# All large backward transfers issued from SyncE in program order, with dV up to eight heads ahead of dK and dq moved forward

## The chip, the cores and the metric

The kernel runs on one core of one Trainium2 chip. The metric is the device time of one execution in microseconds. The core has five engines with an instruction stream of their own (TensorE or PE, VectorE or DVE, ScalarE or ACT, GpSimd or POOL, SyncE or SP) and 16 DMA engines, which move data between the chip's main memory (HBM) and the on-chip memory (SBUF). Any of SyncE, ScalarE and GpSimd can issue a DMA; the issue stands in that engine's stream like any other instruction, and waits there for what it depends on.

## What is computed

One decoding step (one new token for each of B = 4 sequences) of a transformer layer, forward and backward. All tensors are bf16. Attention has H = 32 heads of Dh = 128 and a cache of Sk = 4096 keys and values; D = 512, F = 1792.

```python
def _A_ref(x, k_cache, v_cache, wq, wo):
    q = (x @ wq) split into heads
    scores = einsum("bhqd,bhkd->bhqk", q, k_cache) * Dh ** -0.5
    p = softmax(scores)
    o = einsum("bhqk,bhkd->bhqd", p, v_cache)
    return o.reshape(B, 1, H * Dh) @ wo
def _B_ref(x, w1, w3, w2):
    return (silu(x @ w1) * (x @ w3)) @ w2
h = x + _A_ref(layernorm(x), k_cache, v_cache, wq, wo)
out = h + _B_ref(layernorm(h), w1, w3, w2)
```

The outputs are `out` and the gradients of a loss with the given `grad_out` with respect to x, k_cache, v_cache, wq, wo, w1, w3 and w2. The two cache gradients, dK and dV, have the size of the caches, 134 MB each, and they and the caches make nearly all of the traffic: K is read once, V twice, dK and dV are written once. For each of the 128 pairs of sequence and head (called heads below, s = 0 to 127), with P the softmax row, q the query, dO the gradient of the head's output row, dV = P (outer) dO, dS = P * (V dO - c) * scale, and dK = dS (outer) q.

## The kernel before

**Tiling.** A head's K, V, dK or dV is 4096 rows of 128 numbers, 1 MB in bf16. It lies in SBUF as 128 partitions of 32 rows, 8 KB a partition, in one of 23 equal slots (`NSLOT`, class `Slot`). A slot is taken from the front of the list `free` and given back to its end when the program no longer writes to it; the framework then makes its next user wait until the old one is done. Which slot is used when is thus settled when the program is built.

**Stages.** The forward part (L614 to L676) takes two heads a turn: K and V loads from SyncE, scores, softmax, and per head a 128 x 129 matrix M (sum over the keys of V times P K, and the output column), eight slots `Ms` of 16 heads. Then comes a short middle part (L800 to L924): the feed-forward block and its gradients, dh, the first 8 of 32 head columns of dO, and dV of heads 0 and 1. The rest, from L927, is the backward loop.

**The backward loop (L1218 to L1246).** `front(s)` (L1161) transposes V in four pieces on TensorE (`V_T`, L757; the matmuls are L764, ScalarE's copies back into the same slot L765), and multiplies it with dO (L1177, `dP_ps`; the small stationary `zd` is copied by GpSimd at L1142). Four heads make a group: `rows_out` and `rows_T` bring the group's row through ScalarE (L1152) and TensorE (L1159) into shape, `group_dS` (L1185) makes dS of four heads on VectorE (L1191, L1194). `grad_V(s)` (L777) and `grad_K(s)` (L1197) each take a slot, fill it on VectorE with one outer product (L770, one instruction over 128 x 4096) and store it. They need the rows of dO and q spread over all partitions: `replicate` (L1121; matmuls L1128, ScalarE copies L1131) does that for four heads of both at a time, into two buffers each. dV also needs a doubled copy of P, `P_pairs` (L1144), made by GpSimd at L1147 into three buffers.

Step s of the loop does: load of V ahead, `replicate(s + 4)` in every fourth step, `P_pairs(s + 5)`, `front(s + 5)`, `grad_V(s + 3)`, `grad_K(s)`, in every fourth step `group_dS`, and a piece of other work. V for the backward part lies in a ring of seven slots (`NV2`): a slot goes back to the ring after its head's `front`, and the next load into it is issued one step later.

**Who issues what in the backward part.** V loads: ScalarE (`load_V2(nc.scalar)`, L1206 and L1214). dV stores: GpSimd (L781). dK stores: SyncE (L1201). Stores of weight gradients: GpSimd (L1026, L1069, L1085, L1096). Loads of wq (L961) and w2 (L502): SyncE.

**The other work** is written as generators, and `step(k, n)` runs n pieces. `rest_of_dO` ("o", one piece in each of the steps from `O0` = 2 to 20) transposes the rest of wo, and makes the rest of dO. `side_work` ("s", three pieces in steps 21 to 35, then two) begins with dq: for each of the 128 heads a matmul of M with dO in fp32 (L964), three heads a piece, after which M's slots are given back one by one. Then follow wq transposes and dx, and the weight gradients (`grad_unit`, one matmul and one ScalarE copy at L940 a piece; a slot full of them is stored).

Of the kernel before, what the change touches and what calls it, by code (L numbers as in the profile page):

```python
# [9 lines left out]
FP32 = mybir.dt.float32  # L10
# [14 lines left out]
def kernel(  # L25
# [751 lines left out]
    def grad_V(s):  # L777
# [3 lines left out]
        nc.gpsimd.dma_start(out=rows_of(out_3[b, h]), in_=gv.heads())  # L781
# [145 lines left out]
    with ExitStack() as c2:  # L927
# [22 lines left out]

        def side_work():
# [3 lines left out]
            dq_ps = psx.tile([P, 512], FP32, tag="x2", name="dq_ps")  # L955
            wq2s = deque()

            def load_wq2(cc):
                if cc < DC:
                    wq2s.append(Slot("wq2"))  # L960
                    nc.sync.dma_start(out=wq2s[-1].b(HD), in_=A_wq[cc * P:(cc + 1) * P, :])  # L961

            for s in range(NH):
                nc.tensor.matmul(dq_ps[:, s:s + 1], lhsT=M_of(s)[:, 0:Dh], rhs=dOT_f[:, s:s + 1], start=True, stop=True)  # L964
                if s % MC == MC - 1:
                    Ms[s // MC].give()
                    if s // MC in (3, 5):
                        load_wq2(s // MC // 2 - 1)
                if s % 3 == 2:
                    yield  # L970
# [46 lines left out]
            for cc in range(DC):  # L1017
# [8 lines left out]
                nc.gpsimd.dma_start(out=out_4[cc * P:(cc + 1) * P, :], in_=st.b(HD))  # L1026
# [35 lines left out]
            for i in range(2):  # L1062
# [6 lines left out]
                nc.gpsimd.dma_start(out=out_8[i * 7 * P:(i + 1) * 7 * P, :].rearrange("(p c) j -> p c j", c=7),  # L1069
# [5 lines left out]
            for (rows, out_ap) in ((dg_rows, out_6), (du_rows, out_7)):  # L1075
                for i in range(2):
# [8 lines left out]
                    nc.gpsimd.dma_start(out=out_ap[i * 2 * P:(i + 1) * 2 * P, :].rearrange("(p c) f -> p c f", c=2),  # L1085
# [3 lines left out]
            for h0 in range(0, H, 8):  # L1089
# [6 lines left out]
                nc.gpsimd.dma_start(out=out_5[h0 * P:(h0 + 8) * P, :].rearrange("(p k) j -> p k j", k=8),  # L1096
# [24 lines left out]
        def replicate(i0):  # L1121
            K_ = 8 * B if i0 < 8 * B else P
            for nm_, rows in (("rdo", dOrows_bf), ("rq", qrows_bf)):
                if (nm_, i0 // REP) in reps:
                    continue
                ps = psrep.tile([P, REP, Dh], FP32, tag="rep", name="rep_ps")
                for i in range(REP):
                    nc.tensor.matmul(ps[:, i, :], lhsT=ident_b[0:K_, i0 + i:i0 + i + 1].to_broadcast([K_, P]), rhs=rows[0:K_, :],  # L1128
                                     start=True, stop=True)
# [74 lines left out]
        def prefetch():  # L1204
            while nv["next"] < NH and vring:
                load_V2(nc.scalar)  # L1206
# [70 lines left out]
```

## Time and profile before

| | |
|---|---|
| median of 14 runs | 1716.83 us (1712.33 to 1720.81) |
| the profiled execution | 1714.46 us |
| its span in the profile | 1712.5 us, mean TensorE clock 0.88 |
| busy: PE, DVE, ACT, POOL | 73%, 72%, 57%, 28% of the span |
| moved by DMA | 707.49 MB, mean 413 GB/s |
| read from HBM, written | 422.59 MB, 282.34 MB |
| V loads of the backward part | 119 from ScalarE, 9 from SyncE |
| issue to landing, median | V load 15.6 us, dK store 15.8 us, dV store 29.2 us |
| one dV or dK on VectorE (L770) | 2.30 us, 2.29 us |

The profile gives, for each engine, when each instruction ran and what ended the idle time before it; for the DMA engines, the mean share of time in which they were busy and the rate at which they moved data. The span is cut into 40 equal slices, 42.8 us each: slices 1 to 16 hold the forward part, the hand-over lies in the seventeenth, and the rest is the backward loop. Stretches of time are in us from the start of the span. An engine that is idle costs nothing by itself; what matters is which work ends last, and what it waited for.

### The profile page before, as it was taken

The page shows a single profiled execution, that of the slowest core. Times are in us where ns is not written, and L with a number is a line of the kernel's source. Part 1 is how long each engine was busy: PE and PEld are TensorE (multiplying, and loading weights), DVE is VectorE, ACT ScalarE, POOL GpSimd, SP SyncE. Part 2 cuts the span into 40 slices and gives each one's busy share as a digit, 9 for nine tenths or more (in the row PEclk, how much of TensorE's full clock was granted, in tenths as well). Part 3 has the DMA queues.
Part 4 walks back from the last instruction along what each step waited for, and adds up shares of the span by engine and source line. Part 5 has one row for each costly group of instructions (what it writes and reads, how often), then busy time and mean ns, then how long its engine had stood idle before and what let it go on. Part 6 is the DMA issues. An engine that isn't in the chain of part 4 may idle for free. (4 is left out here: it accounts for less than half of the span.)

```text
span 1712.5 us, 38306 instructions
## 1 busy us (share of the span) xinstructions
PE 1252.7 (73%) x16180; PEld 927.1 (54%) x16180; DVE 1229.2 (72%) x1294; ACT 968.0 (57%) x1502; POOL 471.5 (28%) x822
## 2 busy tenths in 40 slices
PE   5889888888888888766689875665766666656660
PEld 4777677667666666644467754443444433434330
DVE  5989999999998996466767457475556464665684
ACT  3556445444544454676664466675776756656660
POOL 1211232222222221122332244254323131211140
PEclk9999999999999999899886689887797777887895
DMA  9999999999999999799999999999999999999997
GB/s 401 424 424 424 424 424 424 424 423 423 415 424 411 423 408 395 306 394 426 425 426 425 426 386 425 412 425 423 424 423 421 422 409 420 422 422 423 423 425 303
DMA packets 101740, 707.49 MB, mean 413 GB/s; under 512 B 11052, under 2 KB 15288, under 8 KB 17600
## 3 DMA queue, kind: packets, MB, share of 16 engines
q1 hardware_dynamic: 63568, 432.04, 60.5%
q0 software_dynamic: 20864, 148.22, 20.7%
q10 hardware_dynamic: 17136, 124.79, 17.7%
q8 instruction: 127, 2.08, 0.5%
q14 instruction: 45, 0.37, 0.1%
HBM read 422.59 MB, written 282.34 MB: 412 GB/s over the span
## 5 line engine op out<-in xcount | busy, mean ns | idle before, releaser
L765 ACT COPY V<-pt_tps 128x1024 bf16<-128x1024 bf16 x512 | 490.2, 1026 | 166.2 <-PE pt_tps L764 115.2
L764 PE MATMUL pt_tps<-ident_b,V 128*128 128x128 bf16 x4096 | 356.6, 248 | 208.2 <-ACT V L765 202.3
L764 PEld LDWEIGHTS <-V 128*128 128x128 bf16 x4096 | 305.0, 113 | 270.8 <-issue 257.4
L770 DVE TENSOR_TENSOR gv<-P,reps 128x4096 bf16<-128x4096 bf16 x125 | 287.1, 2297 | 129.4 <-DMA out_dram<-gv 110.8
L770 DVE TENSOR_TENSOR gk<-dS,reps 128x4096 bf16<-128x4096 bf16 x128 | 292.7, 2289 | 105.3 <-DMA out_dram<-gv 72.6
L421 DVE TENSOR_TENSOR PK<-Kn,PK 128x4096 bf16<-128x4096 bf16 x128 | 292.3, 2283 | 26.3 <-POOL PK L417 25.9
L436 PE MATMUL M_ps<-PK,Vn 128*128 128x130 bf16 x4096 | 284.1, 221 | 34.9 <-DMA Vn<-in_A_v_cache_dram 34.2
L436 PEld LDWEIGHTS <-Vn 128*128 128x128 bf16 x4096 | 251.8, 99 | 55.3 <-DMA Vn<-in_A_v_cache_dram 47.5
L328 DVE STREAM_TRANSPOSE KT<-Kn 128x512 f32<-128x512 f32 (+1 forms) x321 | 250.6, 797 | 0.3 <-issue 0.2
L1177 PE MATMUL dP_ps<-V,zd 128*32 128x512 bf16 x1024 | 182.3, 440 | 75.2 <-ACT V L765 63.0
L323 ACT COPY KT<-pt_tps 128x1024 bf16<-128x1024 bf16 x128 | 129.5, 1012 | 187.7 <-PE pt_tps L322 154.1
L781 POOL DMA_DIRECT2D out_dram<-gv x128 | 68.2, 533 | 490.3 <-DVE gv L770 464.3
L417 POOL COPY PK<-P_all 128x64 bf16<-128x64 bf16 x128 | 32.4, 253 | 414.9 <-ACT P_all L411 411.9
L334 POOL TENSOR_TENSOR W<-qrep,wmask 128x128 bf16<-128x128 bf16 x128 | 123.6, 966 | 82.3 <-PE S_ps L354 67.7
L1147 POOL COPY P<-P_all 128x64 bf16<-128x64 bf16 x127 | 138.1, 1088 | 0.0
L1177 PEld LDWEIGHTS <-zd 128*32 128x32 bf16 x1024 | 37.6, 95 | 163.3 <-issue 137.2
L1191 DVE TENSOR_SCALAR dPr<-dPT_ps,c_rep 128x32 f32<-128x32 f32 x128 | 23.2, 244 | 131.1 <-PE dPT_ps L1159 130.9
L1142 POOL COPY zd<-dOT_bf 128x2 bf16<-128x2 bf16 x128 | 85.2, 666 | 79.5 <-PE dP_ps L1177 79.5
L1131 ACT CAST reps<-rep_ps 128x512 bf16<-128x512 f32 x62 | 36.3, 586 | 112.7 <-DVE gk L770 74.2
L411 ACT COPY P_all<-pt_P 32x64 bf16<-32x64 bf16 x256 | 51.9, 203 | 53.6 <-PE pt_P L407 51.3
L322 PE MATMUL pt_tps<-ident_b,Kn 128*128 128x128 bf16 x1024 | 80.9, 224 | 0.0
L446 PE MATMUL kP_ps<-PK,onesw 128*32 128x512 bf16 x1024 | 79.1, 386 | 0.0
(244 smaller groups left out, 1359.2 us busy)
## 6 DMA issues: line engine op xcount, KB each, us to landing
Kn<-in_A_k_cache_dram SPq DMA_DIRECT2D x128, 1024.0 KB, 15.5
Vn<-in_A_v_cache_dram SPq DMA_DIRECT2D x128, 1024.0 KB, 15.7
out_dram<-gv POOLq DMA_DIRECT2D x128, 1024.0 KB, 29.2
out_dram<-gk SPq DMA_DIRECT2D x128, 1024.0 KB, 15.8
V<-in_A_v_cache_dram ACTq DMA_DIRECT2D x119, 1024.0 KB, 15.6
V<-in_A_v_cache_dram SPq DMA_DIRECT2D x9, 1024.0 KB, 18.9
wq<-in_A_wq_dram SPq DMA_DIRECT2D x8, 1024.0 KB, 19.5
out_dram<-gw POOLq DMA_DIRECT2D x6, 896.0 KB, 42.2
```

Source lines behind the costliest of these rows:

```text
L322: nc.tensor.transpose(pt[:, i, :], Kn[:, c * GW + i, :], ident_b[:])
L323: nc.scalar.copy(out=KT[:, c * GW:(c + 1) * GW, :], in_=pt[:])
L328: nc.vector.transpose(out=KT[:, c * w_:(c + n) * w_], in_=Kn[:, c * w_:(c + n) * w_])
L334: nc.gpsimd.tensor_tensor(out=W[:, hl], in0=qrep[:, :, s:s + 1].to_broadcast([P, 4, 32]), in1=wmask[:, hl, None, :].to_broadcast([P, 4, 32 ...
L421: nc.vector.tensor_tensor(out=PK[:, :, 0:Dh].rearrange("p j (r t) -> p j r t", t=2), in0=Ks[s].heads().rearrange("p j (r t) -> p j r t", t=2),
L436: nc.tensor.matmul(hold["M"][:], lhsT=Vn[:, j, :], rhs=PK[:, j, :], start=(j == 0), stop=(j == SJ - 1))
L764: nc.tensor.transpose(pt[:, i, :], v[:, g * GW + i, :], ident_b[:])
L765: nc.scalar.copy(out=v[:, g * GW:(g + 1) * GW, :], in_=pt[:])
L770: nc.vector.tensor_tensor(out=dst.rearrange("p j (r t) -> p j r t", t=2), in0=col2[:, :, None, :].to_broadcast([P, SJ, Dh // 2, 2]), in1=r ...
L1142: nc.gpsimd.tensor_copy(out=zd[s % B][:, 32:132:67], in_=dOT_bf[:, s:s + 1].to_broadcast([P, 2]))
L1147: nc.gpsimd.tensor_copy(out=P2s[s][:], in_=P_all[:, s, :, None].to_broadcast([P, SJ, 2]))
L1177: nc.tensor.matmul(rows["acc"][32 * c:32 * (c + 1), :], lhsT=zq_window(zd[hl], 2 * hl + u), rhs=VT[:, j0:j0 + 4, :], start=(hl == 0 and u ...
```

## The change

Three things are changed.

- Where large transfers are issued. The V loads of the backward loop, the dV stores and the weight gradient stores are issued from SyncE, which already issues the dK stores. They stand in its stream in the order in which the program writes them. GpSimd keeps only small DMAs, ScalarE none.
- How far dV runs ahead. `more_V(upto)` makes dV up to a given head. Before the loop it brings dV to head 8, before `group_dS(0)`; in the loop dV leads dK by 8 heads until head 56, then by one less every four heads, down to 3. P and the spread rows of dO follow dV; `replicate` is split, and the rows of q are spread in every fourth step, two steps before they are used.
- When dq is done. The dq matmuls leave `side_work` and become a generator of their own ("q"), four heads a piece, one piece in each of the steps 2 to 34. `side_work` starts at step 35 (`S1`), two pieces a step.

```diff
--- before.py
+++ after.py
@@ -778,7 +778,7 @@
         b, h = bh_of(s)
         gv = Slot("gv")
         outer(gv.heads(), P2s.pop(s), reps["rdo", s // REP][:, s % REP, :])
-        nc.gpsimd.dma_start(out=rows_of(out_3[b, h]), in_=gv.heads())
+        nc.sync.dma_start(out=rows_of(out_3[b, h]), in_=gv.heads())
         if s > 1:
             gv.give()
         else:
@@ -948,26 +948,31 @@
             gu.append((dst, ps, n))
 
 
+        wq2s = deque()
+
+        def load_wq2(cc):
+            if cc < DC:
+                wq2s.append(Slot("wq2"))
+                nc.sync.dma_start(out=wq2s[-1].b(HD), in_=A_wq[cc * P:(cc + 1) * P, :])
+
+        dq_ps = psx.tile([P, 512], FP32, tag="x2", name="dq_ps")
+
+        def dq_work():
+            for s in range(NH):
+                nc.tensor.matmul(dq_ps[:, s:s + 1], lhsT=M_of(s)[:, 0:Dh], rhs=dOT_f[:, s:s + 1], start=True, stop=True)
+                if s % MC == MC - 1:
+                    Ms[s // MC].give()
+                    if s // MC in (5, 6):
+                        load_wq2(s // MC - 5)
+                if s % 4 == 3:
+                    yield
+
+        units["q"] = dq_work()
+
         def side_work():
             pt = psg.tile([P, Dh], BF16, tag="gps", name="pt_O")
             nc.tensor.transpose(pt[:], OT_bf[:], ident_b[:])
             nc.scalar.copy(out=O_sb[:], in_=pt[:])
-            dq_ps = psx.tile([P, 512], FP32, tag="x2", name="dq_ps")
-            wq2s = deque()
-
-            def load_wq2(cc):
-                if cc < DC:
-                    wq2s.append(Slot("wq2"))
-                    nc.sync.dma_start(out=wq2s[-1].b(HD), in_=A_wq[cc * P:(cc + 1) * P, :])
-
-            for s in range(NH):
-                nc.tensor.matmul(dq_ps[:, s:s + 1], lhsT=M_of(s)[:, 0:Dh], rhs=dOT_f[:, s:s + 1], start=True, stop=True)
-                if s % MC == MC - 1:
-                    Ms[s // MC].give()
-                    if s // MC in (3, 5):
-                        load_wq2(s // MC // 2 - 1)
-                if s % 3 == 2:
-                    yield
             yield
             t = rs.f(2080)[:, 1536:1536 + NH]
             nc.vector.tensor_tensor(out=t, in0=c_rep[:], in1=kPT[:], op=ALU.mult)
@@ -1023,7 +1028,7 @@
                               flat.b(HD)[0:B, n8 * 512:(n8 + 1) * 512])
                     yield
                 grad_flush()
-                nc.gpsimd.dma_start(out=out_4[cc * P:(cc + 1) * P, :], in_=st.b(HD))
+                nc.sync.dma_start(out=out_4[cc * P:(cc + 1) * P, :], in_=st.b(HD))
                 st.give()
             flat.give()
             fs.give()
@@ -1066,7 +1071,7 @@
                     grad_unit(st.b(7 * D)[:, k * D:(k + 1) * D], hw[:, k, :], gr_bf)
                     yield
                 grad_flush()
-                nc.gpsimd.dma_start(out=out_8[i * 7 * P:(i + 1) * 7 * P, :].rearrange("(p c) j -> p c j", c=7),
+                nc.sync.dma_start(out=out_8[i * 7 * P:(i + 1) * 7 * P, :].rearrange("(p c) j -> p c j", c=7),
                                   in_=st.b(7 * D).rearrange("p (c j) -> p c j", c=7))
                 st.give()
             oflat = Slot("oflat")
@@ -1082,7 +1087,7 @@
                                       nw[:, k, :], rows[:, f0_:f0_ + w_])
                             yield
                     grad_flush()
-                    nc.gpsimd.dma_start(out=out_ap[i * 2 * P:(i + 1) * 2 * P, :].rearrange("(p c) f -> p c f", c=2),
+                    nc.sync.dma_start(out=out_ap[i * 2 * P:(i + 1) * 2 * P, :].rearrange("(p c) f -> p c f", c=2),
                                       in_=st.b(2 * F).rearrange("p (c f) -> p c f", c=2))
                     st.give()
             r1.give()
@@ -1093,7 +1098,7 @@
                     grad_unit(st.b(8 * D)[:, k * D:(k + 1) * D], ow[:, k, :], dh_bf)
                     yield
                 grad_flush()
-                nc.gpsimd.dma_start(out=out_5[h0 * P:(h0 + 8) * P, :].rearrange("(p k) j -> p k j", k=8),
+                nc.sync.dma_start(out=out_5[h0 * P:(h0 + 8) * P, :].rearrange("(p k) j -> p k j", k=8),
                                   in_=st.b(8 * D).rearrange("p (k j) -> p k j", k=8))
                 st.give()
             oflat.give()
@@ -1118,18 +1123,18 @@
             nc.scalar.copy(out=dh, in_=dr_ps[:])
 
         units["o"] = rest_of_dO()
-        def replicate(i0):
+        def replicate(nm_, i0):
+            if i0 >= NH or (nm_, i0 // REP) in reps:
+                return
             K_ = 8 * B if i0 < 8 * B else P
-            for nm_, rows in (("rdo", dOrows_bf), ("rq", qrows_bf)):
-                if (nm_, i0 // REP) in reps:
-                    continue
-                ps = psrep.tile([P, REP, Dh], FP32, tag="rep", name="rep_ps")
-                for i in range(REP):
-                    nc.tensor.matmul(ps[:, i, :], lhsT=ident_b[0:K_, i0 + i:i0 + i + 1].to_broadcast([K_, P]), rhs=rows[0:K_, :],
-                                     start=True, stop=True)
-                rt = rep_bufs[nm_][i0 // REP % 2]
-                nc.scalar.copy(out=rt, in_=ps[:])
-                reps[nm_, i0 // REP] = rt
+            rows = dOrows_bf if nm_ == "rdo" else qrows_bf
+            ps = psrep.tile([P, REP, Dh], FP32, tag="rep", name="rep_ps")
+            for i in range(REP):
+                nc.tensor.matmul(ps[:, i, :], lhsT=ident_b[0:K_, i0 + i:i0 + i + 1].to_broadcast([K_, P]), rhs=rows[0:K_, :],
+                                 start=True, stop=True)
+            rt = rep_bufs[nm_][i0 // REP % 2]
+            nc.scalar.copy(out=rt, in_=ps[:])
+            reps[nm_, i0 // REP] = rt
 
         rows = {}
         dS2s = {}
@@ -1203,46 +1208,67 @@
 
         def prefetch():
             while nv["next"] < NH and vring:
-                load_V2(nc.scalar)
-
-
-        O0, S0, L, LV = 2, 21, 5, 3
+                load_V2(nc.sync)
+
+
+        O0, S0, S1, L = 2, 21, 35, 5
+        gvd = {"n": 2}
+
+        def more_V(upto):
+            while gvd["n"] < min(NH, upto):
+                s = gvd["n"]
+                P_pairs(s)
+                replicate("rdo", s - s % REP)
+                grad_V(s)
+                P_pairs(s + 1)
+                P_pairs(s + 2)
+                gvd["n"] += 1
+                if s % REP == 2:
+                    replicate("rdo", s + 2)
+
+        def lead_V(s):
+            return 8 - min(5, max(0, s - 56) // 4)
+
 
         def load_ahead(s):
             prefetch()
             if s < NH and s not in V2s and s not in VTs:
-                load_V2(nc.scalar)
+                load_V2(nc.sync)
 
         for s in range(2):
             dO_window(s)
+        for s in range(3, 6):
+            P_pairs(s)
         for s in range(L):
             load_ahead(s)
-            P_pairs(s)
             front(s)
-            if s < 2:
-                first_gv[s].give()
-            elif s < LV + 1:
-                grad_V(s)
+            if s == 0:
+                for gv in first_gv:
+                    gv.give()
+            more_V((4, 6, 7, 8, 9)[s])
+            if s == 0:
+                replicate("rdo", REP)
         group_dS(0)
         for s in range(NH):
             load_ahead(s + L)
-            if s % REP == 0 and s + REP < NH:
-                replicate(s + REP)
-            P_pairs(s + L)
+            if s % REP == 2:
+                replicate("rq", s + 2)
             if s + L < NH:
                 front(s + L)
             elif s + L == NH:
                 rows_out()
                 rows_T()
-            if s > 0 and s + LV < NH:
-                grad_V(s + LV)
+            if s > 0:
+                more_V(s + 1 + lead_V(s))
             grad_K(s)
             if s % B == B - 1 and s + 1 < NH:
                 group_dS((s + 1) // B)
-            if s >= S0:
-                step("s", 3 if s < S0 + 15 else 2)
+            if O0 <= s < S0:
+                step("o")
+            if s >= S1:
+                step("s", 2)
             elif s >= O0:
-                step("o")
+                step("q")
         step("s", 400)
```

## The prediction

> **What bounds the kernel now.** I read the page's forty slices first. From the rows of DMA and GB/s the sixteen DMA engines are busy nearly everywhere, and the full rate is 424 GB/s:
>
> ```profile
> DMA  9999999999999999799999999999999999999997
> GB/s 401 424 424 424 424 424 424 424 423 423 415 424 411 423 408 395 306 394 426 425 426 425 426 386 425 412 425 423 424 423 421 422 409 420 422 422 423 423 425 303
> ```
>
> The bytes don't change with the edit, so what it can win is time in which the DMA engines move less than 424 GB/s. One 1 MB head takes 1.048/424 = 2.47 us, a backward step (one V load, one dV, one dK store) 7.42 us. The windows of 10 us (last columns: granted clock, DMA share, GB/s) show where the backward part falls short. First the hand-over from forward to backward:
>
> ```profile
> 690.00:700.00 10.00, 9.66 (x212) 9.36 (x210) 5.23 (x14) 5.90 (x8) 0.80 (x4) 0.83 0.92 372
> 700.00:710.00 10.00, 6.11 (x76) 4.67 (x73) 6.05 (x6) 4.43 (x7) 3.62 (x16) 0.66 0.74 306
> 710.00:720.00 10.00, 6.74 (x79) 4.07 (x77) 2.29 (x1) 7.49 (x9) 1.47 (x6) 1.00 0.66 252
> 720.00:730.00 10.00, 7.18 (x81) 4.43 (x80) 4.45 (x7) 7.15 (x10) 1.26 (x3) 1.00 0.59 186
> 730.00:740.00 10.00, 7.00 (x84) 4.33 (x82) 8.02 (x4) 7.53 (x9) 4.74 (x6) 1.00 0.95 369
> ...
> 1000.00:1010.00 10.00, 7.87 (x76) 5.93 (x76) 10.00 (x5) 6.96 (x9) 9.96 (x9) 0.67 0.95 346
> 1010.00:1020.00 10.00, 7.72 (x96) 5.18 (x96) 6.89 (x4) 9.37 (x11) 8.01 (x10) 1.00 0.99 366
> ```
>
> Short of 424, the five windows to 740 lack (52+118+172+238+55) x 10/424 = 15.0 us of transfer. Windows 990 to 1020 lack 3.8 us (398, 346, 366), 1090 to 1110 1.2 us (399, 398), 1360 to 1400 1.6 us (409 and 405 over 20 us each). The end, 1696 to 1712.5, lacks some 12 us: all work is issued by 1689, and only the last engines drain. So about 21.6 us lie within the reach of the issue order, at most.
>
> Then I asked for VectorE's order of time in the worst window (start, us, instruction, in brackets its idle time before):
>
> ```profile
> 706.79 2.29 DVE L770 TENSOR_TENSOR gv<-reps 128x4096 bf16<-128x4096 bf16 x1 [3.00 <-PE dP_ps L1177]
> 710.19 2.29 DVE L770 TENSOR_TENSOR gv<-P,reps 128x4096 bf16<-128x4096 bf16 x1 [1.10 <-POOL P L1147]
> 725.27 0.72 DVE L1191 TENSOR_SCALAR dPr<-dPT_ps,c_rep 128x32 f32<-128x32 f32 x4 [12.79 <-PE dPT_ps L1159]
> ```
>
> VectorE makes the stores' data and idles 12.79 us, waiting for TensorE's first four heads, while the DMA engines run at half rate. The dV of later heads needs nothing from TensorE's V path, but the program places only two of them there.
>
> The waits of the whole run and the order of time of TensorE give the second place:
>
> ```profile
> POOL out_dram L781 <- DVE gv L770: 464.3, 98, 13.1
> DVE dPr L1191 <- PE dPT_ps L1159: 130.9, 12, 24.6
> DVE gv L770 <- DMA out_dram<-gv: 110.8, 37, 7.1
> ...
> 970.73 2.37 PE L964 MATMUL dq_ps<-dOT_f,M 128*128 128x1 f32 x18
> 979.04 4.00 PE L964 MATMUL dq_ps<-dOT_f,M 128*128 128x1 f32 x18
> ```
>
> GpSimd's 464 us before L781 are idle and cost nothing by themselves. VectorE waits 130.9 us for TensorE, up to 24.6 us at a time. From 874 us on (21 heads into the loop) TensorE does nine heads of dq a step, 18 passes of 2.37 to 4.00 us; granted clock 0.67 in 892 to 957 and 0.59 in 957 to 996. The distance between group_dS calls (892.08, 957.50, 996.36) is then 8.2 and 9.7 us a head, above 7.42: TensorE sets the pace, stores run dry, and the 990 to 1020 shortfall follows.
>
> **What the Trainium skill says.** "DMA: Bandwidth & Descriptors", section "Issuing engines are not separate DMA queues": all issuers end on the same 16 engines, and spreading only saves issue time. The trace agrees: the forward part, all loads from SyncE, runs at 424, like the backward part from three issuers. Same page, "Queues, rings and completion order": each engine goes round between the rows with work, so today V loads, dV and dK get equal shares, whoever needs them; no view above shows the turn itself, but a dV store takes 29.2 us to land against 15.8 for dK. "SBUF — State Buffer", "Who interferes with whom": a two-input tensor_tensor contends with GpSimd's reads. This trace agrees: the copy of P takes 1088 ns at L1147, beside L770, and its like 253 ns at L417. The copies stay on GpSimd.
>
> **The change, part by part.**
>
> *Issues moved.* 128 dV stores and 14 gradient stores leave GpSimd (0.53 us each), 119 V loads leave ScalarE (0.33 us each, 39 us in 980 us, ScalarE being 60% busy). Worth 0: neither bounds the backward part. SyncE gets them at 0.58 us (two at 695.08 take 1.17): 3 x 0.58 = 1.75 us of each 7.42, hidden. The small loads (dqflat, oflat, the gradient row) stay on GpSimd, with no dV stores in front; worth 0 too.
>
> *SyncE as one line.* Its order is now V(n+12), dV(n+9), dK(n). A V load waits until TensorE has used the buffer (front(n+5)); dV and dK stand behind it, and the next V load stands behind VectorE. A wait costs only once what is already queued has drained. At the start four buffers circulate for dV and dK: three queued writes and one to two loads, 3+1.5 transfers x 2.47 = 11 us, against some 6 us from a landing to the next store (2.3 VectorE, 0.58 issue[...]). Later, as dq and wo give buffers back (one per four heads from step 5), 9 to 13 circulate and it is over 25 us. The 14 gradient stores now make V loads wait for ScalarE; GpSimd waited up to 18.5 us for one (51.0 us for four at L1026), under 25. Bounds 0 and 14 us (1 us for each); I take +3 us.
>
> *dV ahead.* Seven dV (heads 2 to 8) stand before the first group_dS: 7 x 2.29 = 16.0 us from 706.79, to 722.8, within VectorE's idle time. That offers 5 MB more, 12.4 us of transfer, to windows which have (172+238) x 10/424 = 9.7 us free. Not all is won: until 709 the second dV has landed and the third is not made (some 2.4 us); V load 10 waits for front(3) near 725 with dV 8 behind it; V loads 11 and 12 wait for front(4) and front(5), near 730 and 735, as fronts come 5 us apart. The two copies of dO rows (0.58 us each, with four matmuls) now stand between early fronts and delay them 1 to 3 us. I leave 9 us of the 15.0 lost: -6 us, bounds 0 and -10. That gain stays, if the DMA engines are fed afterwards; the lead falls from 8 to 3 over heads 56 to 76, when loads fill in.
>
> On GpSimd the copy of P for a later dV waits for the dV three before it (three buffers), and the copy for zd stands behind; both are then still some four heads ahead of the front that needs zd, so this is worth 0, or 1 us a head if that lead is used up.
>
> *dq spread.* From nine heads of dq a step to four, in steps 2 to 34, beside the wo transposes until step 20. TensorE from 740 to 880 is busy 98.00 us in 140: with a group_dS every 29 us, 5.1 us a head. dq adds 4/9 of 2.37 to 4.00 = 1.1 to 1.8 us; short waits for ScalarE in the packed stretch add 0.6 to 0.9. Sum 6.8 to 7.8, middle 7.3: just under 7.42. So the late bulge goes, and nothing new comes: -3.8 us at 990 to 1020. Bounds 0 and -3.8 as long as TensorE stays under 7.42. Of the other 2.8 us I count half, since in order V no longer loses its turn to a burst of stores: -1.4 us.
>
> *The end.* The last steps keep a dV lead of 3, and VectorE (2.3 us a store) is faster than the DMA: 0.
>
> **The sum.** -6 - 3.8 - 1.4 + 3 = -8.2 us. The profiled execution took 1714.46 (span 1712.5, and 2.0 around it), giving 1706.3; the median of the runs is 2.4 higher, so 1708.6, said as 1709.
>
> **The rivals.**
>
> *TensorE becomes the bound in steps 2 to 34: slower.* For it: the clock fell to 0.59 to 0.67 in the dq stretch, where transposes took 4.1, the dP matmuls with waits 2.2 us; with 1.6 of dq, 1.0 of wo and 0.4 of row copies that is 9.3 us. Against it: dq is a short piece of a step now, and before 880 the clock averaged 0.90. It decides once a step takes over 7.42 us: at 8.0, 33 steps lose 0.58 each, 19 us, and the queue is short there. With the hand-over gain of 6 kept: 1716.8 + 19 - 6 + 1 = 1731. Chance 0.20.
>
> *Given back.* The hand-over gain stays, but one line of issue costs about as much in waits as it wins (14 us at its upper bound less 11 won): 1717. For it: V load and stores have each their own line today and nothing is held up. Against: 11 to 25 us of queued work. Chance 0.14.
>
> *More.* The hand-over loses only 5 of the 15 us (-10), and all 6.6 us later go, without waits: 1716.8 - 16.6 = 1700. Chance 0.10.
>
> **How the numbers follow.** Forecast, 1709, chance 0.56, own range 1704 to 1713. 0.2% (3.4 us) is about what a measurement of this kernel can tell from no change: faster is below 1713.4, slower above 1720.3. Faster 0.56 + 0.10 = 0.66, same 0.14, slower 0.20. The range from 1700 to 1728 takes in the "given back" case and the lighter half of the TensorE case; some 0.10 lies above it and 0.06 below.
>
> **What would show it.** Right: more than 300 GB/s in 710 to 730; VectorE's 12.79 us wait down to under 5; no dip near 1000, dPr waits well under 130.9 us; SyncE's waits for the new stores large without a fall in GB/s. Wrong: slices under 420 GB/s between 740 and 980 with TensorE over 90% busy (the first rival), or dips at side stores with SyncE waiting for ScalarE (the second).

## The result, and the profile after

Below, "before" and "after" name the two kernels, and e1 to e14 the further runs. A line of issue is the row of transfers that one engine issues, in its program order; a transfer has landed when all its parts have arrived; a dip is a stretch in which the DMA engines move clearly less than 424 GB/s.

| | before | after |
|---|---|---|
| median | 1715.45 us (47 runs: the 14 named above and 33 more) | 1702.25 us (10 runs, 1701.42 to 1703.51) |
| ratio to before, 95% interval | | 0.992 (0.9911 to 0.9929) |
| the profiled execution, its span | 1714.46, 1712.5 us | 1703.51, 1701.6 us |
| issue to landing: V load, dV, dK | 15.6, 29.2, 15.8 us | 19.9, 20.0, 20.1 us |
| moved by DMA | 707.49 MB | 707.50 MB |

The kernel became faster by 13.2 us in the medians and by 10.95 us between the two profiled executions; of the ten runs of after the profiled one is the slowest, 1.3 us over their median. The profiles explain the 10.95. The bytes are the same, so the gain is time in which the DMA engines move more. The forty slices of the page after, DMA share and rate:

```profile
DMA  9999999999999999999999999999999999999996
GB/s 401 424 424 423 425 423 425 423 423 423 418 422 409 421 405 398 383 416 424 425 425 426 425 425 426 425 426 426 423 420 421 418 421 415 421 418 417 416 419 282
```

The seventeenth slice, the hand-over, rises from 306 to 383 GB/s; the dips at the 24th and 26th slice (386 and 412 before) are gone. New is that slices 35 to 39 lie at 416 to 421 where they were at 422 to 425.

The hand-over in windows of 10 us (the last two columns are DMA share and GB/s), and a window where the second dip was:

```profile
690.00:700.00 10.00, 9.65 (x201) 9.06 (x200) 4.71 (x14) 6.18 (x8) 0.80 (x4) 0.84 0.91 362
700.00:710.00 10.00, 7.13 (x93) 5.54 (x92) 7.96 (x7) 5.28 (x8) 3.28 (x12) 0.67 0.84 348
710.00:720.00 10.00, 7.23 (x83) 4.52 (x81) 9.47 (x5) 7.72 (x9) 6.77 (x6) 0.96 1.01 416
720.00:730.00 10.00, 7.03 (x79) 4.38 (x78) 6.77 (x9) 7.49 (x10) 4.54 (x6) 1.00 1.01 362
730.00:740.00 10.00, 7.20 (x84) 4.43 (x83) 5.96 (x3) 7.76 (x9) 2.66 (x5) 1.00 1.01 425
1000.00:1010.00 10.00, 6.93 (x83) 4.73 (x82) 5.75 (x8) 6.04 (x7) 2.88 (x4) 0.89 1.02 428
```

Over 690 to 740 the five windows lack (62 + 76 + 8 + 62 - 1) x 10/424 = 4.9 us of transfer, where 15.0 were lacking before. The reason stands in VectorE's order of time:

```profile
706.31 2.29 DVE L770 TENSOR_TENSOR gv<-reps 128x4096 bf16<-128x4096 bf16 x1 [2.01 <-PE dP_ps L1182]
708.52 6.73 DVE L770 TENSOR_TENSOR gv<-P,reps 128x4096 bf16<-128x4096 bf16 x3
715.77 6.73 DVE L770 TENSOR_TENSOR gv<-P,reps 128x4096 bf16<-128x4096 bf16 x3 [0.53 <-POOL zd L1147]
725.66 0.73 DVE L1196 TENSOR_SCALAR dPr<-dPT_ps,c_rep 128x32 f32<-128x32 f32 x4 [3.16 <-PE dPT_ps L1164]
```

Seven dV stand in a row where the 12.79 us of idle time stood; 3.16 us of it are left, and the first group (L1196) starts when it did (725.66, before 725.27). Two kinds of waits of the whole run (total us, times, longest), first VectorE's for the group, then the largest of SyncE's queue:

```profile
DVE dPr L1196 <- PE dPT_ps L1164: 22.5, 8, 6.3
```

```profile
SPq L1206 <- DMA V<-in_A_v_cache_dram: 139.9, 70, 2.8
SPq L781 <- DMA out_dram<-gk: 114.7, 53, 3.3
SPq L797 <- DMA out_dram<-gv: 109.6, 50, 2.8
```

VectorE waits 22.5 us for TensorE instead of 130.9. What the transfers move doesn't explain the waits of SyncE's queue: a dK store (L1206) waits for the landing of a V load, a dV store (L781) for that of a dK. The trace names the semaphore that tells of each landing. The issues of SyncE and ScalarE take eight of them in turn, whichever of the two engines issues, and each waits until the transfer eight places earlier has landed: of the 377 issues after 740 us, 347 start within 0.3 us of that landing, and none before it. So at most eight are under way, and 8 x 2.47 us = 19.8 us is what every transfer now takes to land (19.9 to 20.1). GpSimd's issues have a set of their own. On SyncE this wait holds up no computing. On ScalarE it stands in front of the copies of V (L765), and the waits of the kernel before have it, in a line that the prediction passed over:

```profile
ACT V L765 <- DMA out_dram<-gk: 30.1, 8, 7.4
```

That copy reads nothing of dK. It is ScalarE's next V load, standing ahead of the copy, that waited for a dK store's landing.

**Balance by stretch**, in us of transfer lacking at 424 GB/s (length x (424 - rate)/424):

| stretch | before | after | difference |
|---|---|---|---|
| 690 to 740, hand-over | 15.0 | 4.9 | -10.1 |
| 990 to 1020 | 3.8 (370 GB/s) | 0 (424) | -3.8 |
| 1090 to 1110 | 1.2 (399) | 0 (424) | -1.2 |
| 1110 to 1400 | 2.3 (423, 418) | 1.3 (424, 420) | -1.0 |
| 1400 to 1640 | 1.1 (422) | 4.0 (417) | +2.9 |
| the last 16.5 and 17.6 us | 12.3 | 14.5 | +2.2 |
| the remaining stretches, as the rest | | | +0.1 |

The sum is the difference of the spans, -10.9 us, as the bytes are the same.

**The end.** Windows of 4 us, first before, then after; no compute engine works there, only transfers drain:

```profile
1696.00:1700.00 4.00, 0.00 (x0) 0.00 (x0) 0.00 (x0) 0.00 (x0) 0.00 (x0) 0.50 0.66 277
1700.00:1704.00 4.00, 0.00 (x0) 0.00 (x0) 0.00 (x0) 0.00 (x0) 0.00 (x0) 0.50 0.23 96
1704.00:1708.00 4.00, 0.00 (x0) 0.00 (x0) 0.00 (x0) 0.00 (x0) 0.00 (x0) 0.50 0.14 59
1708.00:1712.00 4.00, 0.00 (x0) 0.00 (x0) 0.00 (x0) 0.00 (x0) 0.00 (x0) 0.50 0.02 10
```

```profile
1684.00:1688.00 4.00, 0.00 (x0) 0.00 (x0) 0.00 (x0) 0.00 (x0) 0.00 (x0) 0.50 0.59 248
1688.00:1692.00 4.00, 0.00 (x0) 0.00 (x0) 0.00 (x0) 0.00 (x0) 0.00 (x0) 0.50 0.06 27
1692.00:1696.00 4.00, 0.00 (x0) 0.00 (x0) 0.00 (x0) 0.00 (x0) 0.00 (x0) 0.50 0.06 27
1696.00:1700.00 4.00, 0.00 (x0) 0.00 (x0) 0.00 (x0) 0.00 (x0) 0.00 (x0) 0.50 0.06 25
```

A share of 0.06 is one sixteenth: after, a single DMA engine is still busy for 12 us when fifteen have finished. More on it below.

### The profile page after: what moved, and what is told of

Read it like the earlier page. It is cut to its first block, busy times and chain, and to the rows that moved or that the text cites. A ratio compares the mean times of both kernels' runs of the same rounds, so it can differ in the third digit from the quotient of the medians.

```text
span 1701.6 us, 38407 instructions
## 1 busy us (share of the span) xinstructions
PE 1238.4 (73%) x16180; PEld 912.7 (54%) x16180; DVE 1236.8 (73%) x1294; ACT 968.0 (57%) x1502; POOL 396.1 (23%) x678
## 2 busy tenths in 40 slices
DMA packets 101741, 707.50 MB, mean 416 GB/s; under 512 B 11052, under 2 KB 15288, under 8 KB 17600
## 4 chain that ended last, share of the span: by engine, by line
DMA 38%; ACT 9%; PE 7%; issue 1%; DVE 1%; DVEq 0%; SPq 0%; ACTq 0%; POOL 0%
DMA out_dram<-gv 15%; DMA V<-in_A_v_cache_dram 11%; ACT V L765 8%; DMA out_dram<-gk 7%; DMA out_dram<-gw 2%; PE pt_tps L764 2%; PE dP_ps L1182 2%; PE dq_ps L962 1%; DMA out_dram<-gwq 1%; DMA wq<-in_A_wq_dram 1%; PE rep_ps L1133 0%; DVE gk L770 0%; PE pt_wo L574 0%; ACT dPr L1157 0%; ACT reps L1136 0%
## 5 line engine op out<-in xcount | busy, mean ns | idle before, releaser
L765 ACT COPY V<-pt_tps 128x1024 bf16<-128x1024 bf16 x512 | 490.0, 1026 | 133.4 <-PE pt_tps L764 128.6
L764 PE MATMUL pt_tps<-ident_b,V 128*128 128x128 bf16 x4096 | 350.5, 246 | 195.1 <-ACT V L765 157.1
L764 PEld LDWEIGHTS <-V 128*128 128x128 bf16 x4096 | 299.9, 112 | 268.2 <-issue 202.4
L1152 POOL COPY P<-P_all 128x64 bf16<-128x64 bf16 x125 | 92.4, 741 | 460.3 <-DVE gv L770 453.0
L1147 POOL COPY zd<-dOT_bf 128x2 bf16<-128x2 bf16 x128 | 131.4, 1027 | 153.7 <-PE dP_ps L1182 153.5
L322 PEld LDWEIGHTS <-Kn 128*128 128x128 bf16 x1024 | 62.3, 100 | 25.6 <-issue 25.6
L386 ACT ACTIVATE E<-S_ps,nm 128x256 f32<-128x256 f32 x64 | 30.3, 474 | 80.0 <-DVE nm L383 80.0
L400 ACT ACTIVATE Pn<-E,rl 128x1024 bf16<-128x1024 f32 x64 | 73.7, 1152 | 3.2 <-DVE rl L397 3.2
## 6 DMA issues: line engine op xcount, KB each, us to landing
Kn<-in_A_k_cache_dram SPq DMA_DIRECT2D x128, 1024.0 KB, 15.6
Vn<-in_A_v_cache_dram SPq DMA_DIRECT2D x128, 1024.0 KB, 15.7
V<-in_A_v_cache_dram SPq DMA_DIRECT2D x128, 1024.0 KB, 19.9
out_dram<-gk SPq DMA_DIRECT2D x128, 1024.0 KB, 20.1
out_dram<-gw SPq DMA_DIRECT2D x6, 896.0 KB, 19.8
wo<-in_A_wo_dram SPq DMA_DIRECT2D x4, 1024.0 KB, 10.8
```

The lines of the kernel that those rows point to most:

```text
L322: nc.tensor.transpose(pt[:, i, :], Kn[:, c * GW + i, :], ident_b[:])
L764: nc.tensor.transpose(pt[:, i, :], v[:, g * GW + i, :], ident_b[:])
L765: nc.scalar.copy(out=v[:, g * GW:(g + 1) * GW, :], in_=pt[:])
L1147: nc.gpsimd.tensor_copy(out=zd[s % B][:, 32:132:67], in_=dOT_bf[:, s:s + 1].to_broadcast([P, 2]))
L1152: nc.gpsimd.tensor_copy(out=P2s[s][:], in_=P_all[:, s, :, None].to_broadcast([P, SJ, 2]))
```

## The experiments

| kernel | median | ratio to before, 95% |
|---|---|---|
| issuers alone (e1) | 1713.81 | 0.9991 (0.9983 to 1.0000) |
| dV ahead alone (e2) | 1706.40 | 0.9952 (0.9939 to 0.9964) |
| dq alone (e3) | 1715.09 | 0.9996 (0.9987 to 1.0005) |
| after with the old issuers (e4) | 1705.44 | 0.9944 (0.9932 to 0.9956) |
| after, V from ScalarE (e5) | 1713.01 | 0.9989 (0.9974 to 1.0005) |
| after, each dq matmul twice (e7) | 1718.27 | 1.0008 (0.9992 to 1.0023) |
| after, lead falls to 3 by step 20 (e8) | 1701.98 | 0.9918 (0.9905 to 0.9932) |
| after, dV and gradient stores from GpSimd (e9) | 1733.81 | 1.0104 (1.0089 to 1.0118) |
| after, small loads behind the end (e10) | 1705.85, one run | |
| after, all dV and dK from GpSimd (e12) | 1709.50 | 0.9959 (0.9947 to 0.9970) |
| after, even heads SyncE, odd GpSimd (e13) | 1747.29 | 1.0182 (1.0161 to 1.0204) |
| after, V from GpSimd (e14) | 1705.60 | 0.9940 (0.9917 to 0.9962) |

The first theory after the result was that dV ahead and the spread dq are the gain and that the single line costs a little. The rival was that the single line is itself the gain. After four runs the theory was that dV ahead gives most of it, at the hand-over, and that the single line matters by the waits that it takes from ScalarE.

**One part at a time.** Issuers alone, which is before with

```diff
-        nc.gpsimd.dma_start(out=rows_of(out_3[b, h]), in_=gv.heads())
+        nc.sync.dma_start(out=rows_of(out_3[b, h]), in_=gv.heads())
...
-                load_V2(nc.scalar)
+                load_V2(nc.sync)
```

and the four lines of gradient stores likewise.

> Only the issuers are changed: V loads, dV stores and gradient stores from SyncE; dV lead of 3 and dq as before. Theory (the gain is the earlier dV at the hand-over and the spread dq, the single line of issue costs a little): about 1717 us, ratio to before 1.000 to 1.003, the window 710 to 730 still near half rate. Rival (the single line in program order is itself the gain): 1709 us or less, ratio 0.996 or less, with the shortfall at 990 to 1110 gone.

Measured: 0.9991, 1713.81 us, between the two expectations. The windows of this run show what came of the two dips, with dq still in its old place:

```profile
880.00:990.00 110.00, 97.35 (x790) 79.05 (x790) 66.11 (x47) 54.71 (x62) 22.32 (x26) 0.69 1.01 425
990.00:1020.00 30.00, 20.91 (x265) 14.82 (x264) 24.73 (x20) 22.05 (x27) 19.72 (x16) 1.00 1.02 425
1090.00:1110.00 20.00, 14.65 (x154) 9.95 (x154) 12.29 (x21) 14.89 (x19) 4.64 (x5) 0.91 1.01 427
1400.00:1640.00 240.00, 160.63 (x1334) 101.81 (x1333) 149.08 (x97) 150.28 (x189) 52.93 (x62) 0.74 1.01 417
```

TensorE is as full in 880 to 990 as before (97.35 us of 110 at a clock of 0.69; before 97.19 at 0.67), and there is no dip after it: 425 where 370 stood. So the dense dq alone doesn't make the dip. The last row gives 417 GB/s back where before had 422; the hand-over, at 291 GB/s, is no better than before (297). That is why the sum is so small.

dV ahead alone is before with `more_V`, `lead_V` and the split `replicate`, old issuers, old dq.

> Only the dV lead of up to eight heads, issued by GpSimd, V loads by ScalarE, dq as before. Theory: the hand-over gains about 10 us, so 1706 us, ratio 0.994 to 0.995, over 400 GB/s in 710 to 720; the shortfall near 1000 stays. Rival (the single line is the gain): no more than 4 us faster, ratio 0.998 or more.

Measured: 0.9952. The rate in 690 to 740 is 374 GB/s against 297, and the dip at 990 to 1020 stays (338 GB/s). Of the 13.2 us, about 8 to 9 come from this part alone.

dq alone is before with `dq_work` in steps 2 to 34 and `S1` = 35.

> Only dq is spread over steps 2 to 34, four heads a piece; issuers and dV lead of 3 as before. Theory: the shortfall of 3.8 us at 990 to 1020 goes, and most of the 1.2 us after it: 1711 us, ratio 0.997 to 0.998, TensorE's clock over 0.85 in 892 to 996. Rival one (TensorE becomes the bound in steps 2 to 34): slower than before, over 1718 us. Rival two (the single line is the gain): 1715 us.

Measured: 0.9996, nothing of the 4 us that the theory expected.

```profile
990.00:1020.00 30.00, 17.59 (x207) 12.26 (x205) 19.21 (x15) 20.21 (x25) 16.07 (x16) 0.90 1.01 422
1090.00:1110.00 20.00, 15.14 (x188) 11.23 (x188) 14.60 (x12) 15.08 (x19) 10.58 (x9) 0.94 0.85 335
```

Before has 370 and 399 GB/s there: the dip wasn't removed, it moved 100 us later.

After with the old issuers takes the reverse of the diff of the first run on the changed kernel, so it holds dV ahead and dq, without the single line.

> The whole change but for the issuers: V loads from ScalarE, dV and gradient stores from GpSimd. Theory: both gains without the cost of one line, 1700 us, ratio to before 0.990 to 0.992, the same as or a little under the changed kernel. Rival (the single line is the gain): 1707 us or more, ratio 0.995 or more.

Measured: 0.9944, 1705.44 us where the theory expected 1700; dq adds next to nothing to dV ahead, and the single line on top of both is worth 1705.44 - 1702.25 = 3.2 us. In this run the dip is at 1090 to 1110 (293 GB/s). ScalarE's order of time there shows how it comes about:

```profile
1088.93 0.33 ACTq L797 DMA_DIRECT2D V<-in_A_v_cache_dram  x1
1089.36 0.58 ACT L1136 CAST reps<-rep_ps 128x512 bf16<-128x512 f32 x1 [15.93 <-DMA wq<-in_A_wq_dram]
1089.84 1.94 ACT L765 COPY V<-pt_tps 128x1024 bf16<-128x1024 bf16 x2
```

and TensorE's in the same run:

```profile
1090.91 1.93 PE L764 MATMUL pt_tps<-ident_b,V 128*128 128x128 bf16 x16 [16.97 <-ACT V L765]
```

ScalarE stands 15.93 us until a wq load of SyncE has landed, which none of its work there reads: its V load (L797) is the instruction that waits. It takes the semaphore of that wq load, which landed at 1088.85 us. The copies of V stand behind it, TensorE waits 16.97 us for them, then VectorE for TensorE, and some 10 us later the DMA engines have less to store. Windows of 10 us read 428, 332 and 254 GB/s from 1080 to 1110. With the V loads on SyncE nothing of ScalarE stands behind them. That this is the single line's gain rests on the runs in which ScalarE issues no V load in the loop: in all of them the stretches from 990 to 1110 lie at 416 GB/s or more.

**TensorE's margin.** The first rival said that TensorE becomes the bound in steps 2 to 34. After with

```diff
-                nc.tensor.matmul(dq_ps[:, s:s + 1], lhsT=M_of(s)[:, 0:Dh], ...
+                for _ in range(2):
+                    nc.tensor.matmul(dq_ps[:, s:s + 1], lhsT=M_of(s)[:, 0:Dh], ...
```

> The changed kernel with every dq matmul done twice (the same result is written again). If the sum of the prediction holds (a step of 6.8 to 7.8 us on TensorE), a step comes to about 8.7 us and 33 steps lose over 1 us each: 1725 us or more. If TensorE has more room, as its 112 us busy of 140 after the change suggest (5.9 us a head, 6.9 with dq twice): 1702 to 1704 us.

Measured: 1718.27 (1709.7 to 1726.3), 16 us above after, and between what the two theories said. Its windows:

```profile
740.00:880.00 140.00, 122.69 (x1129) 96.50 (x1127) 79.12 (x59) 81.96 (x92) 40.31 (x34) 0.74 0.98 386
880.00:990.00 110.00, 96.65 (x844) 76.94 (x844) 67.94 (x52) 58.28 (x67) 37.60 (x29) 0.73 1.00 405
```

After has 111.74 us busy of 140 in the first of these stretches at a clock of 0.93 and 425 GB/s. One more dq of four heads a step brings TensorE to 122.69 us, the granted clock to 0.74, and the rate to 386 and 405. VectorE waits 106.6 us for TensorE's `dPT_ps`, where after has 22.5. So this rival named a mechanism that exists, and its point lies less than one more dq a step away. At 386 and 405 GB/s in place of 424 the two stretches lose 12.5 and 4.9 us. The profiled execution, 1715.42, is 11.9 us above that of after; the stretch 1400 to 1640, at 423 GB/s where after has 417, gives 3.4 us back.

**How long the lead must last.** After with `8 - min(5, s // 4)` in `lead_V`.

> The changed kernel with the dV lead falling from 8 to 3 over steps 0 to 20 and not 56 to 76. If the lead matters only at the hand-over: the same as the changed kernel, 1702 us within 1.5 us. If the standing lead matters: 1705 us or more.

Measured: 1701.98, the same as after. So the lead is needed at the hand-over alone; it can be given back over steps 0 to 20 without loss.

**Half-way divisions of the issues.** V from ScalarE alone (`load_V2(nc.scalar)` in the loop, all stores on SyncE):

> The changed kernel with the V loads back on ScalarE; all stores stay on SyncE. New theory (what the single line is worth is that ScalarE, which TensorE needs for every V piece, no longer waits for finished DMAs before it may issue a V load): a dip under 360 GB/s near 1090 returns, ScalarE waits over 10 us at a time ahead of L797, 1705 us, 2 to 4 us more than the changed kernel. Rival (GpSimd's stores took turns from the V loads): 1702 us, no dip.

Measured: 1713.01, 11 us lost where 2 to 4 were expected. VectorE waits 304.1 us for TensorE's `dPT_ps`, where after has 22.5, as ScalarE's V loads now wait for stores of SyncE. But the rate is 414 to 418 GB/s nearly everywhere from 740 on at a DMA share of 1.00 to 1.01: the DMA engines count as busy and move less.

dV and the gradient stores from GpSimd, V and dK on SyncE:

> The changed kernel with dV and gradient stores back on GpSimd; V loads and dK stores stay on SyncE. New theory: no dip, as ScalarE issues nothing, 1702 us within 1.5 us. Rival (GpSimd's stores took turns from the V loads): 1705 us with a dip.

Measured: 1733.81, far outside what was expected. Two of its windows, with a share of 1.01 and rates of 409 and 402:

```profile
740.00:880.00 140.00, 111.59 (x1247) 82.16 (x1245) 94.58 (x74) 99.02 (x114) 37.90 (x61) 0.91 1.01 409
1110.00:1260.00 150.00, 101.00 (x923) 63.19 (x923) 84.39 (x71) 98.49 (x125) 47.97 (x53) 0.80 1.01 402
```

TensorE isn't late there: it has the 111.6 us of after, and VectorE waits for `dPT_ps` no longer than in after (20.1 us in the whole run). Waits of issue aren't ruled out by the full DMA share: after itself has a share of 1.01 at 362 GB/s in 720 to 730. My next theory was that two lines of unequal demand cost: the lighter one runs dry and restarts (dV lands in 11.9 us here, V and dK in 31). Three runs bear on it. All dV and dK from GpSimd, with V and the gradient stores on SyncE:

> The changed kernel with all dV and dK stores issued from GpSimd, and V loads and gradient stores left on SyncE: two lines again, but now the loads are the lighter one (one third) and the stores the heavier (two thirds); with dV and gradient stores alone on GpSimd the time was 1733.8. Theory A (a lighter line runs dry between transfers and each restart costs the DMA engines time while they count as busy): 1713 to 1736, DMA share at 1.0 and rates of 402 to 418 GB/s in the stretches after 740 us, V landing in 12 us or less and the stores in 25 to 35. Theory B (what cost time was dV or gradient stores from GpSimd in themselves, or writes and reads getting unequal turns by chance): with all stores in one line the order among them is the program's, so within 3 us of 1702, or with slower packets of the stores only. Theory C (a wait of issue: GpSimd's copies of P stand behind stores that wait for VectorE): 1710 to 1730, but with DMA shares under 0.97 where it loses.

Measured: 1709.50, with rates from 407 to 423: a loss of 7 us, not of 31, for the same one to two division, and outside what each of the three theories expected. Even heads on SyncE, odd heads on GpSimd:

```diff
+        (nc.sync, nc.gpsimd)[s % 2].dma_start(out=rows_of(out_3[b, h]), in_=gv.heads())
...
+            (nc.sync, nc.gpsimd)[s % 2].dma_start(out=rows_of(out_2[b, h]), in_=gk.heads())
...
+            (eng, nc.gpsimd)[s % 2 if s > 8 else 0].dma_start(out=V2s[s].heads(), in_=cache_head(A_v_cache, s))
```

> The changed kernel with two equal lines: V, dV and dK of even heads issued from SyncE, those of odd heads from GpSimd (V from head 9 on). Each line holds half of the bytes and the same mixture of reads and writes. Seen so far against 1702 for one line: V alone on ScalarE 1713, dV and gradient stores alone on GpSimd 1734, all stores on GpSimd 1709.5. If it is the unequal demand that costs (a lighter line runs dry and restarts), this one costs little: 1701 to 1706, 422 to 425 GB/s after 740. If lines that mix reads and writes are what costs (the worst case so far, with dK and V on one line, does that), or two lines in themselves, then 1712 to 1735 with 402 to 418 GB/s. If GpSimd's small copies stand behind its V loads, TensorE waits for zd longer than before and the rate falls with the DMA share under 0.97.

Measured: 1747.29, the slowest of all, for two equal lines, and above every range expected. The theory of unequal demand has fallen. The windows:

```profile
740.00:880.00 140.00, 109.68 (x1277) 80.15 (x1277) 97.67 (x75) 100.82 (x117) 49.32 (x73) 0.96 1.01 401
...
1020.00:1090.00 70.00, 39.21 (x452) 28.98 (x450) 37.10 (x21) 38.84 (x44) 14.29 (x35) 0.80 1.01 426
...
1400.00:1640.00 240.00, 140.54 (x1237) 91.16 (x1237) 132.38 (x91) 140.84 (x183) 64.87 (x98) 0.78 0.99 395
```

V from GpSimd, all stores on SyncE:

> The changed kernel with the V loads of the backward loop issued from GpSimd, all stores on SyncE: the same division of bytes as V from ScalarE (1713.0), but GpSimd has semaphores of its own, so that SyncE's stores and the V loads no longer count to the same eight, and ScalarE's copies wait for no issue. If ScalarE's waits made the 11 us: 1701 to 1705. If unequal lines made them: 1708 to 1716, V landing in about 10 us, 414 to 420 GB/s at a DMA share of 1.0. If V loads in GpSimd's line hold up its copies of P and zd: over 1712 with POOL's own waits for V's slots as the sign.

Measured: 1705.60. It divides the bytes as V from ScalarE does and costs 3 us instead of 11. So some 7 us of that run's loss belong to ScalarE as the issuer, with the shared eight; some 3 are left for the two lines.

What the four runs have in common: with loads on one line and stores on the other the loss is 3 to 7 us (e14, e12; e5 with ScalarE's waits besides), and with loads and stores on a line next to a second line it is 31 and 45 us (e9, e13). That is an ordering of the results and not a cause. Within e13 the same division runs at 401 and at 426 GB/s in different stretches, so it isn't the division by itself either. What differs is that at 1020 to 1090 both lines are deep: there GpSimd's transfers take about 30 us to land and SyncE's 40, in 740 to 880 it is 19 to 27 us for both, in 1400 to 1640 GpSimd's take 12 to 17. The number under way doesn't order the rates either: in 740 to 880 it is about 8.7 in e13 (an estimate, the six landing times over the 15.7 us that six transfers of 1 MB take at 401 GB/s), and eight in after, at 425. The records of single packets show where the time goes. A packet of 8 KB takes 309 ns as a rule; over 500 ns take 0.2% of them in after and 5% in e13 in 740 to 880, and 0.1% in e13's fast stretch. Why they take longer, the cause, stays open.

**Who is late at the end.** After with fifteen small loads behind the last store, over 15, 14, ... 1 partitions:

> The changed kernel with fifteen small loads behind the last store, over 15, 14, ... 1 partitions and each of another size, so that the trace tells which of the 16 DMA engines serves which part of a transfer. It is a look at the end of the run, where one engine is still moving data some 12 us after the others, and its time is not meant to be compared: it should be 1702 plus 0 to 10 us. If one engine is late all through (it is a little slower, or has more small packets), then the small loads show it as the same place in each of them, and its packets lie behind those of its neighbours long before the end. If the lateness only comes from the last store, all engines take the small loads at once and none is late by over 3 us.

Measured: 1705.85 in one run. Each of the loads over 15 down to 9 partitions has exactly one packet 2 to 13 us behind its others, while the late engine works off its stores (of the load over 15, all but one packet start within 3.1 us, and one 12.3 us after the next to last). So one of the engines is late for these loads too, and not only with the last store. The Trainium skill, "DMA: Bandwidth & Descriptors", section "Why a DMA increments its semaphore by 16 and not by 1", says that a transfer issued from SyncE over k engines takes the lowest-numbered k, and k is the number of partitions in these loads; with it the late one is among the first nine. No run here shows its number.

How it becomes late is in the sixteen landings of each transfer, one for each engine, as the trace of the changed kernel has them. Relative to the median of the sixteen, in us:

```
median at   first   13th    15th    last
 731.2      -0.3     0.2     0.2     2.6
 909.1      -1.6     1.8     3.4     5.8
1087.9      -3.6     1.0     2.7     8.8
1324.5      -1.9     1.7     3.5    13.4
1503.7      -1.8     0.5     1.3    13.4
1684.6      -1.8     0.6     1.5    13.3
```

From 731.2 to 1324.5 the last engine falls back by 10.8 us in 593, which is 1.8%. After that its distance stays. As each issue waits for all sixteen parts of the eighth transfer before it, no engine can get further ahead than that allows, and all would then run at the pace of the last: 417 GB/s in 1400 to 1640 is 1.7% under 424. The mean distance in 1400 to 1640 is 13.5 to 13.6 us in after, e1 and e8, with one line at 416 to 417 GB/s; in e7, also one line, it is 11.8 us at 423. With the old issuers and dV ahead (e2, e4), at 424 to 425, it is 3.1 and 3.0 us for the transfers of SyncE and ScalarE and 19.7 and 20.0 for GpSimd's dV stores, which wait in a set of their own. So the loss at 1400 to 1640 and the 12 us at the end are probably one thing, a DMA engine that falls 1.8% behind in the backward part. The equality of the two percentages makes this likely; a run that gives that engine fewer bytes would show it, and it wasn't tried.

Whether that engine is slower or has more to carry isn't settled. Alone at the end it moves 25 to 27 GB/s, and a sixteenth of 424 is 26.5. The fetches of instructions, 34 of 16 KB each from 731 to 1325, are not the reason. Around 850 one of them sets one engine back by about 1.4 us, and the next ones set back others, while the last engine's distance also grows between them (from 3.7 us at 865 to 4.6 at 894). The same engine may well have made the wait of 15.93 us in e4 longer: the sixteenth part of that wq load landed 4.8 us after the fifteenth.

## Why the prediction was right, step by step

The direction and the range held. The middle, 1709, was 7 us too high; the sum said -8.2 us, -10.95 came between the profiled executions and -13.2 between the medians. That the sum came out near is in part luck, as errors cancelled: dV ahead won 4 us more than was put down, and the 3.8 us credited to dq came from the issuers. The 3 us put down for waits of the single line did not come as such, but 2.9 us of rate and 2.2 us at the end, which the prediction doesn't have, were lost. The signs that the prediction named for being right came, but for the steady rate in 1400 to 1640, and could not tell these parts apart: e1, without any spreading of dq, also has no dip near 1000.

- **dV ahead: right in mechanism, too small.** -6 was put down with bounds of 0 and -10. -10.1 us came back in the profile, and 8 to 9 us in the run with this part alone. The prediction left 9 us of the 15 lost for three delays (V loads 10 to 12 waiting for fronts, the copies of rows between early fronts, the third dV made late). Only 4.9 us are lost: seven dV were made before the first group, and that group is hardly later (725.66 against 725.27).
- **dq spread: wrong.** The step said that the dense dq, with TensorE above 7.42 us a head, makes the shortfall at 990 to 1020, and that spreading it wins 3.8 us. The shortfall did go, but by another part: with dense dq and the issues on SyncE it is gone (425 GB/s), and with spread dq and the old issuers it comes back at 1090 to 1110 (335 and 293). The chain from a wait of ScalarE's V load to its copies, to TensorE, to VectorE was there to be seen in the waits of the kernel before, where copies of V wait for dK to land, and wasn't read as a wait of issue. Nor does VectorE's longest wait for TensorE, the 24.6 us that the step quoted, belong to dq: it ends at 1092.65 us, in the dip at 1090, and the last dq matmul starts at 998.3.
- **TensorE stays under 7.42 us: right, with little room.** 6.8 to 7.8 us were estimated, waits with it. The busy time in 740 to 880 is 111.74 us over 18.9 heads, 5.9 us a head, and the rate is 425. One dq more of four heads a step breaks it.
- **A single line: the sign was off in part.** +3 us was put down for V loads and stores that hold each other up. These waits are there (`SPq` lines of up to 3.3 us each), and with eight transfers queued they make no dip. What the line wins is that ScalarE no longer waits (the dips, 3.8 + 1.2 us). What it costs is elsewhere: 2.9 us of rate in 1400 to 1640, probably as eight in flight bind all engines to the last one. In sum it is worth 3.2 us on top of the other two parts and 0.0009 x 1715 = 1.5 us alone, the latter hardly more than its uncertainty.
- **Half of the smaller dips, -1.4: they went, in part for another reason.** The dip at 1090 to 1110 (1.2 us) went with the single line, by ScalarE's waits and not by turns among V loads and stores. What removed the one at 1360 to 1400 (1.6 us before) isn't shown: e1 and e4, with and without the single line, have 422 to 425 GB/s there.
- **Issues moved, worth 0: wrong about ScalarE.** The count of 0.33 us an issue was right, and missed that the issue waits. The prediction read the rule that spreading over issuers saves only issue time (the Trainium skill, "DMA: Bandwidth & Descriptors", "Issuing engines are not separate DMA queues") as saying that the choice is free. Here it was not: the same bytes took from 1702 to 1747 us by who issued what.
- **The end, 0: off by 2.2 us.** Not VectorE but one DMA engine ends it; it takes back part of what was won before.

## What to carry to other kernels

An instruction that issues a DMA can wait for a transfer that has nothing to do with it, when semaphores are shared in turn; put large issues where nothing stands behind them, and take a compute engine that waits for a landing which it doesn't read as the sign. A dip in the DMA rate behind a full engine isn't yet caused by it: undo one of the two, and see whether the dip stays or moves. Don't count a half-way division of issues as lying between its two ends: here both ends are good (1705 and 1702), and five kernels between them take 1706 to 1747.

## What the hardware did that was not expected

- A DMA share of 1.0 isn't a full rate: in stretches with a share of 0.99 to 1.01, kernels with two lines of issue moved from 395 to 426 GB/s. With one line it was 416 to 427 in the stretches of after, e1 and e8 from 740 to 1680, and 405 in e7, where TensorE was late. The share counts the time of packets, and in e13's slow stretches 4 to 5% of the packets took over 500 ns, not 309.
- The time from issue to landing follows the number in flight and, with eight in flight, the line's part of the traffic: 8 x 2.47 = 19.8 us with one line (20.0 measured), 8 x 2.47 x 2 = 39.5 us when SyncE's line has half of it (36.9 to 39.1 in e13 over 1400 to 1640).
- One DMA engine of sixteen falls back by about 1.8% from 731 to 1325 us and ends 12 us after the others.
- A doubled dq, four fp32 matmuls a step more, lowers the granted clock in 740 to 880 from 0.93 to 0.74.
